# Turning batch 0's q and k 128 rows at a time, into two banks by position

## The chip, the cores and the metric

The kernel runs on one core of one Trainium2 chip. Its time is the device time of one execution in microseconds; 5 runs of the kernel before gave 304.98 to 306.46 us, with a median of 305.46 us. A smaller time is better. The profile is of one execution, which took 305.09 us as a run; its span, from the program's first to its last instruction, is 303.3 us.

## The reference

Two stages. The first is causal attention with a sliding window of 64 positions, for 8 batches of 8 heads, 576 positions, 64 values a head. The second is a two-layer network with a silu between its layers, over all 4608 tokens.

```python
scores = (1 / sqrt(64)) * q @ k.T                 # per batch and head, 576 x 576
mask   = (rel >= 0) & (rel < 64)                  # rel = query position - key position
attn   = softmax(where(mask, scores, -1e9)) @ v   # 576 x 64
x      = attn, heads side by side                 # 4608 tokens x 512
h      = x @ w_in                                 # 512 -> 2048
out    = (h * sigmoid(h)) @ w_out                 # 2048 -> 512, float32
```

## The kernel before

**Attention.** Scores need q and k with the 64 values of a head on the partitions. Batches 1 to 7 are turned by the vector engine (`turn_blocks`, L248). Batch 0 goes another way, which is the part that the change touches. `two` (L226) reads two heads of q or k as 1152 rows and gives 9 rows that follow each other to each of 128 partitions, so that partitions 0 to 63 hold one head and 64 to 127 the other. The load puts them, as bf16, into a tile `natb` of 128 x 576: by way of `nat` and a cast on ScalarE for the first pair of heads of q and of k (L233, L236), by a casting DMA of the POOL queue for the others (L230). `turn_first` (L276) turns the two tiles of four heads with TensorE matmuls against `ident`, into two PSUM banks, and `lift` (L291) copies each bank to its place in `qt` or `kt`, where the positions of a head lie in order again. There are four turns: q and k of heads 0 to 3 (a = 0) and of heads 4 to 7 (a = 1), each with two lifts.

For batch 0, `scores_first` (L311) adds the window's bias by a matmul (L314) and then multiplies k and q of two heads in halves of the array (L322). `expo` (L340) takes the exponential, `values` (L352) multiplies with v, and `inverse`, `normal`, `to_bridge` (L359, L362, L366) divide, and put the result into `bridge`, the network's input. A unit is one group g of three 64-position blocks and one half a of the heads; batch 0 has six units, n = 0 to 5, and a later batch three double ones. The values of v also need a copy shifted by half a block (`shift_v`, L300 and L302).

**Network.** The tokens go in 9 tiles of 512. `first_layer` (L372) has 16 blocks f of 4 matmuls each, silu (L378) on ScalarE, `second_layer` (L381) 64 matmuls, `copy_out` (L387) and a store. Of tile 0, the first six blocks are computed for 192 tokens and then for the other 320; and its second layer runs with f outermost, so that its 8 pieces of `w_out` (L267, two blocks f each) are needed one after the other. In between stand the scores (L334) and values (L352) of batch 1, three groups of each.

**Order.** The instructions' order on each engine comes from a planner, `Plan.run`, which plays the kernel through with the durations that are given to it and lets each engine take the ready work of the best rank. Work that needs PSUM takes the banks that have been free longest, and TensorE's idle time before batch 0's last exponential is filled with matmuls that nobody reads (`warm`, L586). The turn is entered with 0.7 us of TensorE time (L436), a lift with 0.64 us on ACT or 0.75 us on DVE. Once made, the order is fixed: each engine runs its instructions in turn, and each waits for semaphores.

All loads but the first two go through the POOL queue, in an order that is fixed as well: q and k of batch 0, its v, `w_in` (L261), q and k of batch 1, the first piece of `w_out`, and then v of batch 1 and the other pieces between each other.

Of the kernel before, what the change touches and what calls it, by code (L numbers as in the profile page):

```python
# [9 lines left out]
BF16 = mybir.dt.bfloat16  # L10
# [112 lines left out]
def kernel(ctx, tc, q, k, v, w_in, w_out, out):  # L123
    nc = tc.nc
    B, H, S, D = q.shape
# [11 lines left out]
    NK = 2  # L137
# [5 lines left out]
    NM0, MARGIN = 9, 1.3  # L143
# [8 lines left out]
    ident = keep.tile([128, 128], BF16, name="ident")  # L152
# [8 lines left out]
    natbs = [keep.tile([128, S], BF16, name=f"natb{i}") for i in range(NNB)]  # L161
    qt = [keep.tile([128, NP * S], BF16, name=f"qt{i}") for i in range(NK)]
    kt = [keep.tile([128, 64 + NP * S], BF16, name=f"kt{i}") for i in range(NK)]
# [9 lines left out]
    banks = [psum.tile([128, 512], FP32, name=f"at{i}") for i in range(4)]  # L173
    banks += [psum.tile([128, 512], FP32, name=f"mp{i}") for i in range(4)]

    p = Plan(
        {"at": range(4), "pv": range(4, 6), "mp": range(4, 8), "all": range(8)},
        rank=dict(prime=-8, early=-10, one=-9, first=-9, dma=-1, ld0=-1, st=-2, silu=-3, out=-2, pv=0, s=1, moe=99, warm=200, turn=2,
                  norm=0, inverse=0, bridge=0, exp=1, mask=1, lift=2, block=2, shift=2, cast=4, late=5, clear=9),
        rank0=dict(turn=-6, cast=-6, lift=-5, shift=-4.5, exp=-4, mask=-4, inverse=-3.5, norm=-3, bridge=-3.2),  # L180
        ahead=dict(s=-5.5, exp=-4.6, pv=-5.5, inverse=-4.3, norm=-4.2, bridge=-4.25),
    )
# [31 lines left out]
    def clear_k(i):  # L214
        nc.vector.memset(kt[i][:, 0:64].bitcast(FP32), 0.0)

    c_ident = p.add("one", {"POOL": 1.3}, const_ident)
    c_vv = [p.add("one", {"DVE": 0.25}, lambda _, i=i: clear_vv(i)) for i in range(NV)]
    c_k = [p.add("one", {"DVE": 0.15}, lambda _, i=i: clear_k(i)) for i in range(NK)]
# [9 lines left out]
    def load_first_cast(w, u, kk):  # L229
        nc.gpsimd.dma_start(out=natbs[w][:, 0:S], in_=two(u, kk))  # L230

    def load_first(i, kk):
        nc.sync.dma_start(out=nats[i][:, 0:2 * S].bitcast(FP32), in_=two(0, kk))  # L233

    def cast_first(e, i, w):
        copies[e](out=natbs[w][:, 0:S], in_=nats[i][:, 0:2 * S].bitcast(FP32))  # L236
# [33 lines left out]
        )  # L270


    def at_bf16(op, i=0):
        return banks[op["bank"][i]].bitcast(BF16)[:, 0:S]

    def turn_first(op, ws):  # L276

        for u in range(2):
            for m in range(NM0):
                for j in range(2):  # L280
                    r = slice(64 * j, 64 * j + 64)
                    nc.tensor.matmul(
                        banks[op["bank"][j]].bitcast(BF16)[64 * u:64 * u + 64, 64 * m:64 * m + 64],
                        lhsT=natbs[ws[u]][r, 64 * m:64 * m + 64], rhs=ident[r, r],
                        is_transpose=True, start=(m == 0), stop=(m == NM0 - 1),
                    )

    def place_one(b, pj, kk):
        return kt[b % NK][:, 64 + pj * S:64 + (pj + 1) * S] if kk else qt[b % NK][:, pj * S:(pj + 1) * S]

    def lift(e, op, pj, kk, i):  # L291
        copies[e](  # L292
            out=place_one(0, pj, kk).rearrange("x (p m) -> x p m", m=NM0),
            in_=at_bf16(op, i).rearrange("x (m p) -> x p m", m=NM0),
        )

    def shift_v(e, b, hf, a, z):
# [116 lines left out]
    def add_first_batch():  # L414
        got = {}
        for what, u in FIRST_LOADS:
            if what == "v":
                add_v_loads(0, [u], [c_vv[0]])
                continue
            kk = "qk".index(what)  # L420
            w = n_nat[1] % NNB
            n_nat[1] += 1
            if u == 0:
                i = n_nat[0] % NN
                n_nat[0] += 1
                ld = p.add("ld0", {"SP": 0.45}, lambda _, i=i, kk=kk: load_first(i, kk), dma=-0.15 if kk == 0 else 0.7)
                ca = p.add("cast", {"ACT": 0.7, "DVE": 0.56}, lambda e, i=i, w=w: cast_first(e, i, w), [ld])
                nat_free[i] = [ca]
            else:
                ca = p.add("early" if (what, u) in FIRST_LOADS[2:6] else "dma", {"POOL": 0.6}, lambda _, w=w, u=u, kk=kk: load_first_cast(w, u, kk), dma=0.8)  # L430
            got[what, u] = (w, ca)
            if (what, u ^ 1) not in got:
                continue
            a = u // 2
            ws, loaded = zip(*[got[what, 2 * a + i] for i in range(2)])
            tu = p.add("turn", {"PE": 0.7}, None, [*loaded, c_ident], lat=0.1, pool="all", nb=2)  # L436
            tu["fn"] = lambda _, tu=tu, ws=ws: turn_first(tu, ws)
            for i in range(2):
                x = 2 * a + i
                tu["untils"][i].append(p.add("lift", {"ACT": 0.64, "DVE": 0.75}, lambda e, tu=tu, x=x, kk=kk, i=i:  # L440
                                             lift(e, tu, x, kk, i), [tu, c_k[0]]))
                kq_done[(0, a)] = kq_done.get((0, a), []) + tu["untils"][i]

    def add_w_out(which):
# [23 lines left out]
    def add_v_loads(b, parts, busy):  # L468
        v_landed.setdefault(b, []).extend(
            p.add("dma", {"POOL": 1.0}, lambda e, part=part: load_v(e, b, part), busy, dma=1.1, lat=MARGIN * (b > 0)) for part in parts)  # L470
# [61 lines left out]
    def add_tile(j):  # L532
# [46 lines left out]
        free_gt.update(uses)  # L579

    add_first_batch()
    add_batch_v(0)


    def warm(op):
# [4 lines left out]
                 pool="all")  # L590
# [52 lines left out]
```

The softmax here doesn't subtract the row's maximum and nothing guards it: scores larger than these inputs give would overflow.

## Time and profile before

| | |
|---|---|
| median of 5 runs | 305.46 us (304.98 to 306.46) |
| the profiled execution, as a run | 305.09 us |
| its span | 303.3 us |
| mean granted TensorE clock | 0.994 |
| TensorE busy | 290.2 us (96%), 3635 matmuls |
| ScalarE, VectorE, POOL busy | 172.1, 137.2, 125.6 us |
| the turn's matmuls (L282) | 144, from 4.93 to 11.86 us |
| lifts (L292) on ACT | 5, of 627 to 645 ns |
| lifts (L292) on DVE | 3, of 758 ns |
| first layer of tile 0 (L372) | from 21.92 us on |
| first layer of tile 1 (L372) | from 56.92 us on |

The times below are counted from the start of the span. A row of the timeline holds its start, the time it covers, the engine, the line, the operation, what is written and read, and how many instructions were merged in it; in brackets stands the idle time of the engine just before it and what ended it. "issue" is idle time in which the engine waited for nothing that the profile shows. "PEld" are TensorE's weight loads, one for each matmul, which overlap the matmuls.

### The profile page before, as it was taken

To read this page: it belongs to the slowest core of one execution; us is meant where nothing else is said; L and a number is where in the kernel's file an instruction comes from. 1 tells how busy PE (TensorE), PEld (TensorE's weight loads), DVE (VectorE), ACT (ScalarE), POOL (GpSimd) and SP (SyncE) were. 2 spreads that over 40 slices of the span, in tenths; PEclk is the share of its full clock that TensorE was granted. 3 is DMA by queue.
4 is the path that set the end of the run, shared out by engine and by line. 5 is a ranking of instruction groups with operands and counts; after the bars stand their busy time and mean duration, and the time that the engine had idled before them with its cause. 6 is when DMAs were issued, how large, how long until landed. Compare 5 with 4: busy or idle time off the path is not lost.

```text
span 303.3 us, 8484 instructions
## 1 busy us (share of the span) xinstructions
PE 290.2 (96%) x3635; PEld 144.3 (48%) x3635; DVE 137.2 (45%) x329; ACT 172.1 (57%) x314; POOL 125.6 (41%) x177
## 2 busy tenths in 40 slices
PE   4959998999999999999999999999999999999996
PEld 2537444654544454445444454445445544444444
DVE  2465557753998198706970786065105520000000
ACT  4856662577357834774387628663767366226611
POOL 8967985958979997993320000000000000000000
PEclk9998999999999999999999999999999999999999
DMA  8999999999999999999390111001001110110012
GB/s 171 158 183 162 128 174 170 157 185 88 148 184 128 132 143 177 144 134 113 76 101 2 38 71 37 1 37 71 37 0 39 62 44 0 37 69 36 2 69 71
DMA packets 115238, 28.64 MB, mean 94 GB/s; under 512 B 104704, under 2 KB 110464, under 8 KB 115200
## 3 DMA queue, kind: packets, MB, share of 16 engines
q0 software_dynamic: 109440, 18.07, 79.0%
q1 hardware_dynamic: 5760, 10.03, 9.1%
q8 instruction: 28, 0.46, 0.7%
q14 instruction: 10, 0.08, 0.1%
HBM read 36.70 MB, written 9.44 MB: 152 GB/s over the span
## 4 chain that ended last, share of the span: by engine, by line
PE 92%; issue 3%; DMA 2%; POOL 1%; ACT 1%; DVE 1%; POOLq 0%; ACTq 0%
PE mp L372 42%; PE mp L381 42%; PE at L334 3%; PE mp L352 3%; DMA vv<-in_v_dram 2%; PE at L352 1%; POOL natb L230 1%; ACT e L340 0%; ACT g L378 0%; DVE kt L292 0%; DVE vv L302 0%; PE mp L314 0%; DVE vv L300 0%; PE mp L322 0%; POOL ident L189 0%
## 5 line engine op out<-in xcount | busy, mean ns | idle before, releaser
L381 PE MATMUL mp<-w_out_sb,g 128*128 128x512 bf16 (+2 forms) x608 | 130.2, 368 | 0.2
L372 PE MATMUL mp<-bridge,w_in_sb 128*128 128x512 bf16 (+3 forms) x624 | 129.3, 366 | 0.5 <-ACT g L378 0.4
L378 ACT ACTIVATE g<-mp 128x512 bf16<-128x512 f32 (+3 forms) x156 | 86.3, 564 | 37.0 <-PE mp L372 36.1
L372 PEld LDWEIGHTS <-w_in_sb 128*128 128x128 bf16 x624 | 61.6, 99 | 66.6 <-issue 6.6
L381 PEld LDWEIGHTS <-g 128*128 128x128 bf16 x608 | 55.8, 98 | 61.0 <-issue 0.3
L387 ACT COPY ot<-mp 128x512 f32<-128x512 f32 (+2 forms) x36 | 20.1, 562 | 64.7 <-PE mp L381 51.5
L343 DVE TENSOR_TENSOR e<-e,mask 128x384 bf16<-128x384 bf16 x84 | 25.9, 347 | 62.4 <-ACT e L340 61.6
L340 ACT ACTIVATE e<-at 128x384 bf16<-128x384 f32 x88 | 36.5, 496 | 19.0 <-PE at L334 18.7
L240 POOL DMA_DIRECT2D nat<-in_k_dram x56 | 38.5, 711 | 13.1 <-DMA vv<-in_v_dram 6.9
L240 POOL DMA_DIRECT2D nat<-in_q_dram x56 | 37.8, 696 | 3.8 <-DMA w_in_sb<-in_moe_w_in_dram 2.0
L255 POOL DMA_DIRECT2D vv<-in_v_dram x32 | 33.0, 1055 | 9.6 <-PE mp L352 9.6
L366 DVE STREAM_TRANSPOSE bridge<-ox 128x384 bf16<-128x384 bf16 x48 | 24.7, 551 | 0.1
L248 DVE STREAM_TRANSPOSE qt<-nat 128x576 bf16<-128x576 bf16 x28 | 19.8, 745 | 4.3 <-DMA nat<-in_q_dram 4.3
L248 DVE STREAM_TRANSPOSE kt<-nat 128x576 bf16<-128x576 bf16 x28 | 19.7, 742 | 1.3 <-DMA nat<-in_k_dram 1.3
L362 DVE TENSOR_TENSOR ox<-mp,rc 128x384 bf16<-128x384 f32 x37 | 18.3, 535 | 0.1
L352 PEld LDWEIGHTS <-e 128*32 128x32 bf16 x1152 | 11.0, 95 | 14.4 <-issue 12.2
L359 DVE RECIPROCAL rc<-mp 128x6 f32<-128x6 f32 x37 | 6.9, 190 | 16.2 <-PE mp L352 15.6
L302 DVE COPY vv<-vv 64x576 bf16<-64x576 bf16 (+1 forms) x13 | 8.5, 654 | 10.1 <-DMA vv<-in_v_dram 9.8
L334 PE MATMUL at<-qt,kt 32*128 32x64 bf16 x1008 | 11.8, 190 | 0.2 <-ACT e L340 0.2
L334 PEld LDWEIGHTS <-kt 32*128 32x128 bf16 x1008 | 9.4, 92 | 4.6 <-issue 3.7
L352 PE MATMUL mp<-vv,e 128*32 128x65 bf16 x888 | 10.4, 194 | 0.0
L340 ACT ACT_TABLE_LOAD x7 | 9.0, 1283 | 2.2 <-PE at L334 2.1
(50 smaller groups left out, 86.5 us busy)
## 6 DMA issues: line engine op xcount, KB each, us to landing
out_dram<-ot SPq DMA_DIRECT2D x35, 256.0 KB, 2.1
vv<-in_v_dram POOLq DMA_DIRECT2D x32, 144.0 KB, 5.8
nat<-in_q_dram POOLq DMA_DIRECT2D x56, 72.0 KB, 4.2
nat<-in_k_dram POOLq DMA_DIRECT2D x56, 72.0 KB, 4.0
w_out_sb<-in_moe_w_out_dram POOLq DMA_DIRECT2D x8, 256.0 KB, 7.1
w_in_sb<-in_moe_w_in_dram POOLq DMA_DIRECT2D x6, 256.0 KB, 7.8
w_in_sb<-in_moe_w_in_dram POOLq DMA_DIRECT2D x4, 128.0 KB, 5.4
natb<-in_q_dram POOLq DMA_DIRECT2D x3, 144.0 KB, 4.7
```

What stands on the lines that cost most here:

```text
L240: nc.gpsimd.dma_start(out=nats[i][32 * h:32 * h + 32].rearrange("p (r d) -> p r d", r=NR), in_=(q, k)[kk][b, 4 * a + h].rearrange("(r p) d ...
L248: nc.vector.transpose(out=to[:, 2 * a * S:2 * a * S + 2 * S].rearrange("x (s r t) -> x s r t", s=2, r=NR)[:, :, n * part:n * part + n], in ...
L255: queue[e].dma_start(out=vv[b % NV][:, 2 * g0 + 1:2 * g1 + 1:2, 0:D], in_=v[b].rearrange("h s d -> (h s) d").rearrange("(g p) d -> p g d", ...
L334: nc.tensor.matmul(at_six(op["bank"][h])[:, a, x], lhsT=kt[b % NK][r, at:at + 128], rhs=qt[b % NK][r, at:at + 64], start=(s == a == x == 0 ...
L340: nc.scalar.activation(out=es[n % NE], in_=at_six(bank), func=ACTF.Exp, scale=scale)
L343: nc.vector.tensor_mul(es[n % NE], es[n % NE], mask0 if g == 0 else mask)
L352: nc.tensor.matmul(at_pv(bank)[32 * h:32 * h + 32, x, t], lhsT=e_of(b, a, n, h)[:, x, 32 * t:32 * t + 32], rhs=vv[b % NV][:, (4 * a + h) * ...
L366: nc.vector.transpose(out=bridge[:, n0:n0 + 3, 2 * a:2 * a + 2].rearrange("x t s (u i) -> x t s u i", u=2), in_=oxs[n % NOX].rearrange("p ...
L372: nc.tensor.matmul(banks[bank["bank"][0]][:, lo:hi], lhsT=w_in_sb[:, c, ft * 128:(ft + 1) * 128], rhs=bridge[:, (j * TT + lo) // 64:(j * T ...
L378: nc.scalar.activation(out=gts[gt][:, lo:hi], in_=banks[bank["bank"][0]][:, lo:hi], func=ACTF.Silu)
L381: nc.tensor.matmul(banks[bank["bank"][0]][:, 0:hi - lo], lhsT=gts[gt][:, m * 128:(m + 1) * 128], rhs=w_out_sb[:, f, lo:hi], start=(f == 0) ...
L387: copies[e](out=ots[ot][:, lo:hi], in_=banks[bank["bank"][0]][:, 0:hi - lo])
```

## The change

The two banks of a turn no longer hold two heads each, but all four heads for a part of the positions: the first bank takes the rows m = 0 to 4 of each partition's nine, the second m = 5 to 8. One matmul turns all 128 partitions, two heads, of one m, where before it turned 64. A turn so has 18 matmuls with 128 columns each in place of 36 with 64, and the two `natb` tiles now alternate, where before the first was finished ahead of the second. A lift copies 128 x 640 or 128 x 512 values in place of 128 x 576, and writes them 9 values apart, where before it wrote in order and read 64 values apart. The turn is entered into the planner with 0.6 us in place of 0.7.

```diff
-    def at_bf16(op, i=0):
-        return banks[op["bank"][i]].bitcast(BF16)[:, 0:S]
+    HALVES = ((0, 5), (5, NM0))
+
+    def turned(op, i):
+        lo, hi = HALVES[i]
+        return banks[op["bank"][i]].bitcast(BF16)[:, 0:128 * (hi - lo)].rearrange("x (m y) -> x m y", y=128)
 
     def turn_first(op, ws):
 
-        for u in range(2):
-            for m in range(NM0):
-                for j in range(2):
-                    r = slice(64 * j, 64 * j + 64)
+        for i, (lo, hi) in enumerate(HALVES):
+            for m in range(lo, hi):
+                for u in range(2):
                     nc.tensor.matmul(
-                        banks[op["bank"][j]].bitcast(BF16)[64 * u:64 * u + 64, 64 * m:64 * m + 64],
-                        lhsT=natbs[ws[u]][r, 64 * m:64 * m + 64], rhs=ident[r, r],
-                        is_transpose=True, start=(m == 0), stop=(m == NM0 - 1),
+                        turned(op, i)[64 * u:64 * u + 64, m - lo], lhsT=natbs[ws[u]][:, 64 * m:64 * m + 64], rhs=ident,
+                        is_transpose=True, start=(m == lo), stop=(m == hi - 1),
                     )
 
-    def place_one(b, pj, kk):
-        return kt[b % NK][:, 64 + pj * S:64 + (pj + 1) * S] if kk else qt[b % NK][:, pj * S:(pj + 1) * S]
-
-    def lift(e, op, pj, kk, i):
+    def lift(e, op, a, kk, i):
+        to = kt[0][:, 64:] if kk else qt[0]
         copies[e](
-            out=place_one(0, pj, kk).rearrange("x (p m) -> x p m", m=NM0),
-            in_=at_bf16(op, i).rearrange("x (m p) -> x p m", m=NM0),
+            out=to[:, 2 * a * S:2 * a * S + 2 * S].rearrange("x (j p m) -> x m j p", j=2, m=NM0)[:, HALVES[i][0]:HALVES[i][1]],
+            in_=turned(op, i).rearrange("x m (j p) -> x m j p", j=2),
         )
...
-            tu = p.add("turn", {"PE": 0.7}, None, [*loaded, c_ident], lat=0.1, pool="all", nb=2)
+            tu = p.add("turn", {"PE": 0.6}, None, [*loaded, c_ident], lat=0.1, pool="all", nb=2)
             tu["fn"] = lambda _, tu=tu, ws=ws: turn_first(tu, ws)
             for i in range(2):
-                x = 2 * a + i
-                tu["untils"][i].append(p.add("lift", {"ACT": 0.64, "DVE": 0.75}, lambda e, tu=tu, x=x, kk=kk, i=i:
-                                             lift(e, tu, x, kk, i), [tu, c_k[0]]))
+                tu["untils"][i].append(p.add("lift", {"ACT": 0.64, "DVE": 0.75}, lambda e, tu=tu, a=a, kk=kk, i=i:
+                                             lift(e, tu, a, kk, i), [tu, c_k[0]]))
```

## The prediction

> **What bounds the kernel now.** I read the page first, then TensorE's timeline up to 60 us, where the change can act, then the DMA issues there, and last the built programs' order, before and after.
>
> ```profile
> span 303.3 us, 8484 instructions
> ...
> PE   4959998999999999999999999999999999999996
> ...
> PEclk9998999999999999999999999999999999999999
> DMA  8999999999999999999390111001001110110012
> ...
> q8 instruction: 28, 0.46, 0.7%
> ...
> PE 92%; issue 3%; DMA 2%; POOL 1%; ACT 1%; DVE 1%; POOLq 0%; ACTq 0%
> ```
>
> TensorE sets the end (92% of the chain that ended last) and is full from the fourth slice on. The DMA engines are as full for the first 19 slices (some 144 us). So early on TensorE may be early and yet have to wait for a load. The dip in slice 3 (15 to 23 us) and the stretch from 37 to 56 us show where it does not flow:
>
> ```profile
> 17.21 0.29 PE L352 MATMUL at<-vv,e 128*32 128x65 bf16 x13
> 21.12 0.27 PE L352 MATMUL at<-vv,e 128*32 128x65 bf16 x11 [3.62 <-issue]
> ...
> 37.24 0.81 POOL L267 DMA_DIRECT2D w_out_sb<-in_moe_w_out_dram  x1
> 37.39 2.30 PE L381 MATMUL mp<-w_out_sb,g 128*128 128x512 bf16 x9
> ...
> 43.45 0.55 PE L334 MATMUL at<-qt,kt 32*128 32x64 bf16 x48
> ...
> 44.13 1.24 PE L381 MATMUL mp<-w_out_sb,g 128*128 128x512 bf16 x5
> ...
> 45.80 0.52 PE L334 MATMUL at<-qt,kt 32*128 32x64 bf16 x45 [0.20 <-ACT e L340]
> ...
> 46.25 1.25 PE L381 MATMUL mp<-w_out_sb,g 128*128 128x512 bf16 x5
> ...
> 48.68 0.43 PE L352 MATMUL at<-vv,e 128*32 128x65 bf16 x31
> ...
> 50.05 0.31 PE L352 MATMUL at<-vv,e 128*32 128x65 bf16 x17 [0.95 <-issue]
> ...
> 50.30 4.92 PE L381 MATMUL mp<-w_out_sb,g 128*128 128x512 bf16 x22
> ```
>
> Two things are to be seen. Two stops by "issue" lie in the middle of a run of equal matmuls, which wait for no semaphore there. And 44.13 is a landing: the fourth piece of w_out is issued at 37.24, and the DMA issues of that window give it 6.8 us to landing, so 44.1 (its semaphore is full at 44.09).
>
> **The two stops.** Counted in TensorE's program, they lie before instructions 706 and 1474, which are 768 = 3 x 256 apart. Queue q8 brought 28 packets of 16 KB for 7278 TensorE instructions, 260 each. So TensorE's program comes in blocks of 256, which begin at 194, 450, 706, 962, 1218, 1474 and so on. The packet of the first stop ran from 18.77 to 19.74 and TensorE went on at 21.12, that of the second from 47.72 to 48.67 and 50.05: in both 1.38 us after its end. The time from the start of one block's work to when the block after it could run (packet's end + 1.38) was 6.8 (block 450), 6.7, 3.8 (block 962, begun at 38.45), 4.2 (block 1218, at 45.83) and 4.9 us (block 1474). Where 256 instructions last less than this, TensorE stops. After the first stop the clock was at half for 3.4 us (21.81 to 25.23; the mean from 21.1 to 26 is 0.65).
>
> [...]
>
> **The change, part by part.** *Turns.* 72 of 144 matmuls go. 36 took 0.66 us at full clock (11.20 to 11.86), in pairs of different rows of the array: 18 pairs of 64 columns. The new 18 are 9 pairs of 128 columns, so the same 1152 columns in turn if the pairs, which now differ in the array's columns, still overlap. L352's groups differ in the same way, 4 at a time: 48 matmuls of 65 columns took 0.49 us, where one after another they would take 48 x 65 x 0.424 ns = 1.32 us (a filler of 384 columns every 0.163 us gives 0.424). So 0, at worst 18 x 128 x 0.424 = 0.98 in place of 0.49: +0.5 a turn, +1.0 at the slow pace of the first two (1.10 and 0.99 us). I take 0, the nearer row.
>
> [...]
>
> *First turn.* Its second matmul now reads the second tile, which lands at 5.30: up to 0.4 us later than the start at 4.93.
>
> *Lifts.* Eight as before. On ACT 0.64 us for 576 and 0.50 for 384 values make 0.69 for 640; on DVE 0.76 x 512/576 = 0.67. No row writes 2-byte values 18 bytes apart. Bounds: 0.5 (the 384-value row) and, as an estimate, twice the L292 rows, 1.3 and 1.5 us. I take 0.7. Queued behind the lifts are ACT's exponentials and DVE's shifts of v.
>
> *What hides these.* The lifts of k's second half stand behind the shift of v on DVE, which waits for v's landing at 12.33 (5.93 + 6.4), as now. Then the first layer needs w_in's sixth piece (issued 13.37, semaphore full at 20.79), and the second layer w_out's second piece (32.80 + 4.8 = 37.6). POOL's and SP's programs are unchanged, and none of these loads waits for TensorE. Without this cover each microsecond late would count in full.
>
> *Order.* Up to the first layer TensorE, ACT and DVE are reordered; from there on TensorE's program is the same but for bank numbers, 140 instructions earlier (637 in place of 777). So the blocks begin 140 instructions later in the work. Block 450 now begins in the values of n = 2, 706 in the first layer, 962 at the second scores of batch 1, 1218 in its first values, 1474 in its third.
>
> **The sum.** Without the stop at 17.5 the values of batch 0 end near 18.2, 3.6 us earlier. The 192-token blocks wait for w_in at 20.8, the 320-token ones for the last transpose to bridge: DVE's eight steps behind the last values, some 4.5 us, so 22.9. A late block 450 or 706 can add a microsecond or two; I put block 706 at 24 to 25. Then 14 x 0.134 + 40 x 0.215 + 8 x 0.215 = 12.2 us bring the second piece of w_out into use at 36.2 to 37.2; it lands at 37.57. Before, it was used at 39.10. Third piece: 34.51 + 6.3 = 40.8, before used at 41.41. Fourth: 44.1, before used at 44.13. So the 3.6 us, and 1.7 of half clock, are all gone at 44.13. What is left is gained behind it, and its cause is that the second scores, before the landing and not held by it, run at 42.55 in place of 43.44, with their exponentials:
>
> - 5 matmuls of L381, 1.08: 45.21
> - third scores, now without the wait until 45.80 for exponentials, 0.48: 45.69
> - 3 matmuls, 0.65: 46.34; fifth piece of w_out (38.98 + 7.4) 46.42; 2 matmuls, 0.43: 46.85
> - first values with 0.1 of changeover, 0.59: 47.44
> - 3 matmuls, 0.65, and second values, 0.59: 48.68
>
> The shifts of v (landed 45.06) end near 45.9 and the second exponentials near 44.9, in time. Before, the same point is 50.30, so 1.62 us are gained: 0.47 before the values and 1.15 at the stop of block 1474. The later pieces land at 47.64, 48.88 and 50.48, ahead of their use (48.9 on). From 50.3 on TensorE was full, and the chain that follows moves as a whole.
>
> Whether a new stop takes the old one's place is decided by block 1218: block 962 begins at 42.55, and 1218 is wanted at 47.25, 4.7 us later. The nearest rows in time are 3.8 and 4.2, the farthest 6.8: no stop, at worst 2.1. I take none. Block 1474 is wanted 6.55 us after that.
>
> 305.09 - 1.62 = 303.47 for a run like the profiled one, which stands 0.37 under the median: **303.8 us**.
>
> **Rivals.** *A stop in the new place.* Block 1218 is 0.3 to 1.7 us late (5.0 to 6.4 us after 962): gain 0 to 1.3, some 304.7 us. For it: 6.7 and 6.8 among the rows. Against: both come from before 28 us, where w_in is loaded.
>
> *The whole early gain arrives*: 3.62 + 1.7 = 5.3, so 300.1 us. For it: the stop is on the chain. Against: w_out's landings, which POOL's order fixes.
>
> *Slower, by late blocks twice.* At X us a block, the stop is X - 4.7 at 1218 and X - 6.55 at 1474. Above X = 6.9 the two take more than the gain and 0.9 us besides; at 7.5 they take 2.8 + 0.95, so 307.6 us. For it: 6.8 is close, and weight pieces of 256 KB are in the queues then. Against: no row is over 6.8.
>
> *The early gain is not made*, because the new lifts or turns are slow: at their upper bounds the path is some 3 us longer, the second piece is used at 39 to 40 us, and about 305.3 comes out.
>
> **How the numbers follow.** No difference within 0.3% (0.92 us) can be told from this kernel's spread. Forecast 0.52, a stop in the new place 0.22, early gain not made 0.09, slower 0.13, whole gain 0.04. Faster by more: nearly all of the first, a third of the second, the last, 0.58; slower 0.13; the rest, 0.29, the same. The range from 303.0 to 305.7 leaves out the whole gain, most of slower and a little more; the likeliest case alone has 303.0 to 304.4.
>
> **What would show it.** After: no issue gap before the first layer of 3 us, which begins at 18 to 20 us, and no half clock there; L381's fourth piece still at 44.1; the second scores at 42 to 43; second values ending near 48.7, first layer of tile 1 at 55.3 in place of 56.92. An issue gap inside L352 between 47 and 49 us is the second rival. The prediction is wrong if the landing near 44.1 moves, or if the lifts take over 1.5 us.

## The result, and the profile after

The change made the kernel slower, by 0.36% (the ratio of the runs), where the forecast had it 0.5% faster.

| | before | after | predicted |
|---|---|---|---|
| median, us | 305.98 (80 runs) | 307.55 (43 runs) | 303.8 |
| ratio to before, 95% interval | | 1.0036 [1.0022, 1.0049] | 0.995 |
| profiled execution, as a run | 305.09 | 307.09 | 303.47 |
| its span | 303.3 | 305.3 | |
| lifts on ACT (640 values) and DVE (512) | | 2.95 to 3.32, 2.40 to 2.62 | 0.7 |
| first layer of tile 0 | 21.92 | 24.90 | 18 to 20 |
| second piece of w_out first used | 39.10 | 42.05 | 37.6 |
| second layer goes on after batch 1's second values | 50.30 | 52.12 | 48.7 |
| first layer of tile 1 | 56.92 | 58.74 | 55.3 |

Seven of the 43 runs lie between 305.66 and 306.04, the others between 306.8 and 308.6; why they part stays open. The difference of the medians is 1.57 us, and 0.36% is 1.1 us.

The page of the kernel after (the 40 slices are of 7.6 us):

```profile
span 305.3 us, 8339 instructions
...
PE   4668999999999999999999999999999999999996
...
PEclk9979999999999999999999999999999999999999
...
PE 91%; ACT 5%; DVE 2%; POOL 1%; issue 1%; POOLq 0%; ACTq 0%
PE mp L380 41%; PE mp L371 40%; PE at L333 3%; PE mp L351 3%; ACT qt L291 2%; ACT kt L291 2%; ACT e L339 1%; PE at L351 1%; DVE bridge L365 1%; POOL natb L230 1%; DVE ox L361 1%; PE at L284 0%; PE at L584 0%; ACT g L377 0%; PE at L313 0%
```

In the chain that ended last, "issue" has gone from 3% to 1%: the stops are away, as was meant. ACT has gone from 1% to 5%, and 2% and 2% of it are the lift, L291. TensorE's dip lies in slices 1 to 4 now, and the clock falls in the third (0.72 on average from 19 to 25 us). The groups of L291, each with the least, the median and the greatest duration in ns and the first and last start, and below them what waited for them:

```profile
L291 ACT COPY qt<-at x2: 3025/3171/3317, 6.0 to 11.4; 128x640 bf16<-128x640 bf16 x2
L291 DVE COPY qt<-at x2: 2467/2544/2622, 6.4 to 11.1; 128x512 bf16<-128x512 bf16 x2
...
L291 DVE COPY kt<-at x1: 2401/2401/2401, 15.5 to 15.5; 128x512 bf16<-128x512 bf16 x1
L291 ACT COPY kt<-at x1: 2946/2946/2946, 16.0 to 16.0; 128x640 bf16<-128x640 bf16 x1
...
  PEld L321: 4.5, 2
  PE at L321: 3.7, 2
```

Not 0.7 us but 2.4 to 3.3, some 4.7 ns a value on either engine. The scores, L321, wait for them. The chain of waits from 4 to 30 us (start, time, what) shows how they lie one behind the other on ACT:

```profile
6.00 3.02 ACT qt L291
9.02 2.82 ACT kt L291
11.84 2.83 ACT qt L291
14.68 1.43 ACT e L339 x4
16.10 2.85 ACT kt L291
```

13 us pass on ACT from the first lift to the end of the last, and the exponentials stand behind the third of them. In this chain an ACT lift takes 2.82 to 3.02 us; the records of 3.31 and 3.32 begin some 0.5 us before the lift ahead of them ends. TensorE's timeline has the rest:

```profile
9.26 0.69 PE L284 MATMUL at<-ident,natb 128*64 128x128 bf16 x18
...
11.90 0.35 PE L321 MATMUL at<-qt,kt 64*128 64x64 bf16 x12 [1.51 <-ACT kt L291]
...
19.00 0.43 PE L321 MATMUL at<-qt,kt 64*128 64x64 bf16 x12 [2.20 <-ACT kt L291]
...
24.90 3.17 PE L371 MATMUL mp<-bridge,w_in_sb 128*128 128x192 bf16 x26
...
40.34 2.30 PE L380 MATMUL mp<-w_out_sb,g 128*128 128x512 bf16 x9
...
46.89 1.25 PE L380 MATMUL mp<-w_out_sb,g 128*128 128x512 bf16 x5
...
52.12 4.92 PE L380 MATMUL mp<-w_out_sb,g 128*128 128x512 bf16 x22
...
58.74 1.47 PE L371 MATMUL mp<-bridge,w_in_sb 128*128 128x256 bf16 x12
```

The first layer begins 2.98 us later than before. All of w_out's pieces are there by the time they are used (the fourth is used at 46.89 and landed at 43.53), so there is nothing left in which the lateness could be lost: 2.95 us at the second piece. The stop of block 1474 is gone, as predicted, and gives 1.15 back: 2.95 - 1.15 = 1.80, and 1.82 is what the rows have, 52.12 against 50.30 and 58.74 against 56.92. The span is 2.0 us longer.

### The profile page after: what moved, and what is told of

The parts are those of the page before. It is cut to its first block, busy times and chain, and to the rows that moved or that the text cites. A ratio compares the mean times of both kernels' runs of the same rounds, so it can differ in the third digit from the quotient of the medians.

```text
span 305.3 us, 8339 instructions
## 1 busy us (share of the span) xinstructions
PE 291.6 (96%) x3564; PEld 143.4 (47%) x3564; DVE 143.1 (47%) x330; ACT 180.4 (59%) x313; POOL 125.2 (41%) x177
## 4 chain that ended last, share of the span: by engine, by line
PE 91%; ACT 5%; DVE 2%; POOL 1%; issue 1%; POOLq 0%; ACTq 0%
PE mp L380 41%; PE mp L371 40%; PE at L333 3%; PE mp L351 3%; ACT qt L291 2%; ACT kt L291 2%; ACT e L339 1%; PE at L351 1%; DVE bridge L365 1%; POOL natb L230 1%; DVE ox L361 1%; PE at L284 0%; PE at L584 0%; ACT g L377 0%; PE at L313 0%
## 5 line engine op out<-in xcount | busy, mean ns | idle before, releaser
L371 PEld LDWEIGHTS <-w_in_sb 128*128 128x128 bf16 x624 | 60.2, 97 | 67.9 <-issue 7.9
L339 ACT ACTIVATE e<-at 128x384 bf16<-128x384 f32 x90 | 37.5, 498 | 18.8 <-PE at L333 18.7
L240 POOL DMA_DIRECT2D nat<-in_k_dram x56 | 37.3, 675 | 9.7 <-DMA vv<-in_v_dram 3.3
L361 DVE TENSOR_TENSOR ox<-mp,rc 128x384 bf16<-128x384 f32 x39 | 19.4, 536 | 0.1
L351 PE MATMUL mp<-vv,e 128*32 128x65 bf16 x936 | 11.4, 195 | 0.0
L301 DVE COPY vv<-vv 64x576 bf16<-64x576 bf16 (+1 forms) x14 | 7.6, 544 | 3.2 <-DMA vv<-in_v_dram 2.9
```

Of the source, the lines that this page charges most:

```text
L240: nc.gpsimd.dma_start(out=nats[i][32 * h:32 * h + 32].rearrange("p (r d) -> p r d", r=NR), in_=(q, k)[kk][b, 4 * a + h].rearrange("(r p) d ...
L339: nc.scalar.activation(out=es[n % NE], in_=at_six(bank), func=ACTF.Exp, scale=scale)
L351: nc.tensor.matmul(at_pv(bank)[32 * h:32 * h + 32, x, t], lhsT=e_of(b, a, n, h)[:, x, 32 * t:32 * t + 32], rhs=vv[b % NV][:, (4 * a + h) * ...
L361: nc.vector.tensor_mul(oxs[n % NOX], at_pv(bank)[:, :, :, 0:D], rcs[n % NRC].unsqueeze(3).to_broadcast([128, 3, 2, D]))
L371: nc.tensor.matmul(banks[bank["bank"][0]][:, lo:hi], lhsT=w_in_sb[:, c, ft * 128:(ft + 1) * 128], rhs=bridge[:, (j * TT + lo) // 64:(j * T ...
```

## The experiments

Two questions: is it the lift's output pattern alone, and would the rest of the sum have held without it? The first four kernels ran on one chip, 12 times each (the second of them 5 times), beside 29 runs of the kernel before with a median of 305.87 us.

**Dense writes.** Here batch 0's q and k keep the order of the bank in which they were turned, so that its scores are of other positions than the reference's; all else is the kernel after.

```diff
-            out=to[...].rearrange("x (j p m) -> x m j p", j=2, m=NM0)[:, HALVES[i][0]:HALVES[i][1]],
+            out=to[...].rearrange("x (m j p) -> x m j p", j=2, m=NM0)[:, HALVES[i][0]:HALVES[i][1]],
```

> The changed kernel, its lifts writing their values one after the other (q and k of batch 0 so stay in the order of the bank, and batch 0's scores are of other positions than the reference's). Theory, the 2-byte writes 18 bytes apart are what costs (4.7 ns a value on both engines): lifts fall from 2.4 to 3.3 us to 0.6 to 0.75 us, the first layer begins at 18 to 20 us, the fourth piece of w_out still sets 44 us, and the rest of the prediction's sum is seen: 303.5 to 304.5 us. Rival, the new turn or the reading of its banks costs: lifts stay over 2 us and the time near 307.

Measured: 304.41 us, ratio 0.9949 [0.9926, 0.9972]. The groups of the lift's line:

```profile
L291 ACT COPY qt<-at x2: 692/692/692, 5.8 to 10.1; 128x640 bf16<-128x640 bf16 x2
L291 DVE COPY qt<-at x2: 424/424/425, 6.2 to 10.5; 128x512 bf16<-128x512 bf16 x2
```

The same number of values, from the same banks, in 692 and 424 ns. The input's pattern and the turns are as in the kernel after, so the distance between the writes is the cost. The 0.69 that the prediction worked out for ACT is what a dense write takes.

**The old turn with writes apart.** The opposite: the kernel before, with the two loops of its lift swapped, so that it reads in order and writes 9 values apart.

```diff
-            out=place_one(0, pj, kk).rearrange("x (p m) -> x p m", m=NM0),
-            in_=at_bf16(op, i).rearrange("x (m p) -> x p m", m=NM0),
+            out=place_one(0, pj, kk).rearrange("x (p m) -> x m p", m=NM0),
+            in_=at_bf16(op, i).rearrange("x (m p) -> x m p", m=NM0),
```

> The kernel before, with its turns, banks and instruction order; only a lift's two inner loops are swapped, so that it reads its bank in order and writes 9 values apart, and gives the same result. Theory, writes apart cost 4.7 ns a value: lifts take 2.6 to 2.9 us instead of 0.64 and 0.76, and the time is 1 to 4 us over before. Rival, the new turn or its banks cost: lifts as before and no change of the time.

Measured: 311.43 us, ratio 1.0176 [1.0139, 1.0213].

```profile
L292 ACT COPY kt<-mp x2: 3017/3027/3037, 9.3 to 11.9; 128x576 bf16<-128x576 bf16 x2
...
L292 DVE COPY kt<-at x1: 2693/2693/2693, 18.7 to 18.7; 128x576 bf16<-128x576 bf16 x1
```

Without any of the change's turns, the lifts go from 0.64 and 0.76 us to 2.7 and 3.0. The pattern alone makes the loss. The 5.5 us are more than was expected: this kernel still has the stop before instruction 706 (here 3.49 us, from 25.54 to 29.03), behind its late lifts; how the 5.5 divide was not followed further.

**Runs of neighbours.** The kernel after, with the position m as the innermost loop on both sides. The same values go to the same places, in runs of 5 or 4 neighbours.

```diff
-            out=to[...].rearrange("x (j p m) -> x m j p", j=2, m=NM0)[:, HALVES[i][0]:HALVES[i][1]],
-            in_=turned(op, i).rearrange("x m (j p) -> x m j p", j=2),
+            out=to[...].rearrange("x (j p m) -> x j p m", j=2, m=NM0)[:, :, :, HALVES[i][0]:HALVES[i][1]],
+            in_=turned(op, i).rearrange("x m (j p) -> x j p m", j=2),
```

> The changed kernel with a lift's loops in another order: it writes runs of 5 (or 4) neighbouring values and then leaves out 4 (or 5), and reads 128 values apart. Same result. Theory, what costs is that each 2-byte write starts a place of its own: about a fifth to a quarter of 4.7 ns a value or the usual 1.1 to 1.3, whichever is more, so 0.7 to 1.0 us a lift and 303.5 to 304.8 us. Rival, two engines write between each other's values in the same rows: that is still so, so lifts stay at 2.4 us or more and the time near 307.

Measured: 304.34 us, ratio 0.9939 [0.9917, 0.9962]. It beats both kernels: it is the change as it should have been written. Its lifts, and then its timeline:

```profile
L291 ACT COPY qt<-at x2: 752/752/752, 5.9 to 10.2; 128x640 bf16<-128x640 bf16 x2
L291 DVE COPY qt<-at x2: 719/722/725, 6.3 to 10.4; 128x512 bf16<-128x512 bf16 x2
```

```profile
18.66 0.95 PE L371 MATMUL mp<-bridge,w_in_sb 128*128 128x192 bf16 x8
...
38.64 0.38 PE L380 MATMUL mp<-w_out_sb,g 128*128 128x512 bf16 x1 [2.44 <-DMA w_out_sb<-in_moe_w_out_dram]
...
42.34 1.89 PE L380 MATMUL mp<-w_out_sb,g 128*128 128x512 bf16 x8 [1.23 <-DMA w_out_sb<-in_moe_w_out_dram]
...
45.48 1.24 PE L380 MATMUL mp<-w_out_sb,g 128*128 128x512 bf16 x5 [0.77 <-DMA w_out_sb<-in_moe_w_out_dram]
...
50.04 4.92 PE L380 MATMUL mp<-w_out_sb,g 128*128 128x512 bf16 x22
```

The first layer begins at 18.66, and TensorE then stands 2.44, 1.23 and 0.77 us before three pieces of w_out: the early gain is lost there, as the prediction had it. No stop by issue is in the second layer. In this one execution the loads were about 1 us late (the second piece landed at 38.60, before at 37.57), so 50.04 is 0.26 earlier than before; the dense kernel, whose loads were sooner (the second piece landed at 37.82), is at tile 1 at 56.03 against 56.92, 0.89 earlier:

```profile
44.33 1.24 PE L380 MATMUL mp<-w_out_sb,g 128*128 128x512 bf16 x5 [0.81 <-DMA w_out_sb<-in_moe_w_out_dram]
...
47.16 0.59 PE L380 MATMUL mp<-w_out_sb,g 128*128 128x512 bf16 x2 [0.36 <-DMA w_out_sb<-in_moe_w_out_dram]
...
56.03 1.91 PE L371 MATMUL mp<-bridge,w_in_sb 128*128 128x256 bf16 x16
```

For what the gain is worth the medians must serve: 305.87 - 304.34 = 1.53.

**Blocks moved.** The kernel before, with nothing of the change, but with 58 small matmuls that nobody reads ahead of all others. They and their weight loads are 116 instructions and shift the blocks of 256.

```diff
+    pre = keep.tile([128, 64], BF16, name="pre")
+    nc.vector.memset(pre, 0.0)
+    for i in range(58):
+        r = slice(32 * (i % 4), 32 * (i % 4) + 32)
+        nc.tensor.matmul(banks[7][r, 0:32], lhsT=pre[:, 0:32], rhs=pre[:, 32:64], start=True, stop=True)
```

> The kernel before with 58 small matmuls that nobody reads (116 instructions) put ahead of its first one, in TensorE's idle time up to 4.2 us: the blocks of 256 instructions then begin at the same places of the work as in the changed kernel, and lifts are as before. Theory, the two stops lie where a block begins that is late: the stops of 3.6 and 1.0 us go, and the time is 1.0 to 1.8 us under before (304.2 to 305.0). Rival, the stops belong to the place in the work: they stay within the values of n = 4 and of batch 1's second group, and the time stays.

Measured: 304.25 us, ratio 0.9944 [0.9923, 0.9965]. TensorE's timeline:

```profile
18.49 0.19 PE L322 MATMUL at<-qt,kt 64*128 64x64 bf16 x1 [1.24 <-issue]
...
43.80 1.24 PE L381 MATMUL mp<-w_out_sb,g 128*128 128x512 bf16 x5 [0.82 <-DMA w_out_sb<-in_moe_w_out_dram]
...
46.94 0.59 PE L381 MATMUL mp<-w_out_sb,g 128*128 128x512 bf16 x2 [0.66 <-DMA w_out_sb<-in_moe_w_out_dram]
...
49.19 4.92 PE L381 MATMUL mp<-w_out_sb,g 128*128 128x512 bf16 x22
```

The stop before instruction 706 is there still, in front of other work (batch 0's scores) and of 1.24 us in place of 3.62; so it sits at a place in the program and not at a matmul. The one before 1474 is gone. The expectation that both go was met by half. The time is that of the repaired change: with the old turns and more matmuls than before, moving the boundaries gives 1.6 us as well (305.87 - 304.25). That the added matmuls bring TensorE to its full pace sooner is not what gives it: the third turn takes 0.99 us here (from 9.69 on), in the kernel before 0.66 (from 8.47 on). That the turns are fewer is worth nothing of itself that these runs can tell.

**The copies by themselves.** The kernel before, with copies of 256 values behind its end, first on DVE, then on ACT, then on both. From L619 to L625 only the output's distance changes:

```diff
+    nc.vector.tensor_copy(out=pa[:, 0:256], in_=banks[0].bitcast(BF16)[:, 0:256])
...
+    nc.vector.tensor_copy(out=pa[:, 0:2304].rearrange("x (n s) -> x n s", s=9)[:, :, 0:1], in_=banks[0].bitcast(BF16)[:, 0:256].rearrange("x (n r) -> x n r", r=1))
...
```

> The kernel before with copies of 256 values from PSUM, and one from SBUF, added behind its end, one at a time on DVE and then on ACT: 2-byte values written one after the other, 4, 8, 16, 18, 32 and 64 bytes apart, in runs of 2 and 4 values 18 bytes apart, 4-byte values one after the other and 36 bytes apart; and last two pairs with both engines writing 18 bytes apart at once. Theory, what costs is a write of less than a whole word of some size: 18 bytes apart takes some 4.7 ns a value (1.2 us for 256) on an engine alone, also 4 bytes apart, runs of 2 and 4 are cheaper by their length, and 4-byte values apart cost little more than together. Rival, the two engines take the time from each other: alone about half, 0.6 us, and 1.2 us in the pairs. Second rival, the distance itself costs: 4-byte values 36 bytes apart cost as much as 2-byte values, and 64 bytes apart costs more than 8.

The time of this one execution, 326.9 us, is longer by the added copies. Its timeline: on DVE L619 is dense, L620 to L623 write 4, 8, 16 and 18 bytes apart, L626 and L627 runs of 2 and 4 values every 18 bytes, L628 and L629 4-byte values, dense and 36 bytes apart. On ACT L635 writes 18 bytes apart. L645 and L646 do so on both engines at once.

```profile
301.37 0.29 DVE L619 COPY pa<-at 128x256 bf16<-128x256 bf16 x1 [51.88 <-PE at L618]
301.70 0.44 DVE L620 COPY pa<-at 128x256 bf16<-128x256 bf16 x1
302.17 0.72 DVE L621 COPY pa<-at 128x256 bf16<-128x256 bf16 x1
302.93 1.29 DVE L622 COPY pa<-at 128x256 bf16<-128x256 bf16 x1
304.26 1.27 DVE L623 COPY pa<-at 128x256 bf16<-128x256 bf16 x1
...
308.12 0.62 DVE L626 COPY pa<-at 128x256 bf16<-128x256 bf16 x1
308.78 0.43 DVE L627 COPY pa<-at 128x256 bf16<-128x256 bf16 x1
309.25 0.42 DVE L628 COPY pa<-at 128x256 f32<-128x256 f32 x1
309.71 0.61 DVE L629 COPY pa<-at 128x256 f32<-128x256 f32 x1
...
314.12 1.28 ACT L635 COPY pa<-at 128x256 bf16<-128x256 bf16 x1
...
322.62 1.27 ACT L646 COPY pb<-at 128x256 bf16<-128x256 bf16 x1
...
322.82 1.27 DVE L645 COPY pa<-at 128x256 bf16<-128x256 bf16 x1
```

Three readings. For 2-byte values from PSUM written 4 bytes apart or more the two engines pay the same (on ACT 0.44, 0.72, 1.29 and 1.28 us at 4, 8, 16 and 18 bytes), and at 18 bytes also together (L645 and L646), so they don't hinder each other; that rival falls. The price grows with the distance up to 16 bytes and is flat from there (at 32 and 64 bytes 1.23 and 1.27 us); my theory that any distance costs 4.7 ns a value was wrong at 4 bytes, 0.44 us. And a 2-byte value 18 bytes apart costs twice what a 4-byte value 36 bytes apart does (1.27 us against 0.61 for 256).

From L620 to L622 follows a fit: 256 values touch 64, 128 and 256 stretches of 16 bytes, the distance from which the price is flat, and 0.16 us + 4.4 ns a stretch gives 0.44, 0.72 and 1.29. It meets the lifts that it was not made from, where single values are written 18 bytes apart: 512 values 2.41 (2.40 to 2.62 measured), 576 values 2.69 (2.69 to 3.04 in the old turn with writes apart), 640 values 2.98 (2.95 to 3.32); the longest of each overlap the copy ahead of them. The lifts in runs of 4 or 5 neighbours lie over 144 stretches, 0.79 by the fit and 0.72 and 0.75 measured. Elsewhere it fails. Runs of 2 lie over 144 stretches too, and took 0.62; the 4-byte values 36 bytes apart touch 256, 1.29 by the fit and 0.61 measured. Nor has it a term for the input: the kernel before writes densely and reads 128 bytes apart, 0.48 by the fit for 72 stretches and 0.76 measured on DVE. So it is a fit for single 2-byte values and no mechanism; why they cost this stays open.

**Lifts on DVE alone.** The kernel after, with ACT taken out of the lift; one execution.

```diff
-                tu["untils"][i].append(p.add("lift", {"ACT": 0.64, "DVE": 0.75}, lambda e, tu=tu, a=a, kk=kk, i=i:
+                tu["untils"][i].append(p.add("lift", {"DVE": 0.75}, lambda e, tu=tu, a=a, kk=kk, i=i:
```

> The changed kernel with all eight lifts on DVE. Theory, a write 18 bytes apart costs 4.7 ns a value on one engine alone: 2.4 us for 512 and 3.0 us for 640 values, eight in a row, so some 21 us of lifts on DVE, and 2 to 6 us more than the changed kernel. Rival, the engines hinder each other: some 1.2 and 1.5 us, and the time falls to that of before or under it.

Measured: 314.57 us, beside 305.97 for the kernel before. One group of the lift's line:

```profile
L291 DVE COPY qt<-at x4: 2624/2810/3199, 6.5 to 19.3; 128x640 bf16<-128x640 bf16 x2, 128x512 bf16<-128x512 bf16 x2
```

With ACT out of the way a lift on DVE takes no less than before, so the rival of hindrance falls in the kernel too. Eight of them one after another last to 27.6 us, and the time, 7 us over the kernel after, is above what was expected.

**w_out sooner.** The runs of neighbours, with w_out's third and fourth pieces ahead of more of batch 1's v.

```diff
-    FIRST, SECOND_LOADS = 6, "awbwvwvvwv"
+    FIRST, SECOND_LOADS = 6, "awbwwvwvvv"
```

> The kernel of e3 with one change in the order of POOL's loads: the third piece of w_out is asked for ahead of v's first quarter of batch 1, and the later ones so too. Theory, after the lifts are repaired the early gain is held back by w_out's landings alone: the second layer's waits for pieces 3 and 4 (1.6 and 0.9 us in e3) shrink by about 1 us each, v's later quarters come about 1 us later but ahead of their use near 48 us, and the time falls by 0.3 to 1.2 us against e3, to 303.2 to 304.1 us. Rival, the loads as a whole set the time there, and their order doesn't matter: 304.0 to 304.8 us, with the wait moved to v or to the last pieces.

Measured, on another chip than the kernel that it changes: 304.15 us (12 runs), ratio 0.9957 [0.9929, 0.9985]. In TensorE's timeline the waits for the third and fourth piece are gone, and one is new before the fifth:

```profile
46.64 0.59 PE L380 MATMUL mp<-w_out_sb,g 128*128 128x512 bf16 x2 [1.16 <-DMA w_out_sb<-in_moe_w_out_dram]
```

The wait moved, and the ratio lies within the interval of the order that it replaced. Whether another order can bring the early gain through stays open.

## Why the prediction was wrong

**Turns: right.** A turn of the kernel before, and one of the kernel after with its weight loads:

```profile
11.20 0.66 PE L282 MATMUL at<-ident,natb 64*64 64x64 bf16 x36
```

```profile
9.26 0.53 PEld L284 LDWEIGHTS <-natb 128*64 128x64 bf16 x18 [0.32 <-issue]
9.26 0.69 PE L284 MATMUL at<-ident,natb 128*64 128x128 bf16 x18
```

18 matmuls in 0.69 us at a granted clock of 1.00, before 36 in 0.66: fewer instructions and the same columns, nothing won and nothing lost. The 18 weight loads take 0.53 us of the same 0.69, beside the matmuls. The first turn waited 0.18 for its second tile; up to 0.4 was allowed.

**Lifts: the step that failed.** "I take 0.7", with 1.3 and 1.5 as the upper bound. It was 2.4 to 3.3. The value was scaled by the count of elements from rows that write in order, and the upper bound was twice such a row, with nothing under the two. The text itself says that no row writes 2-byte values 18 bytes apart; a bound that no row supports should have been wider, or been replaced by asking what the pattern does. The sign that it gave for being wrong, lifts of over 1.5 us, came. That it is the output's distance and nothing else of the change was shown by taking it away (dense, runs) and by adding it to the old turn. In the copies by themselves, 256 2-byte values on DVE cost 0.72 us already at 4 values apart, against 0.29 dense; 4-byte values 36 bytes apart pay as well, but far less: 0.61 against 0.42.

**Cover: fell with it.** I named the landings of w_in and w_out as the work that hides the lifts, to 20.8 and 37.6 us. How much they hide is seen in the runs of neighbours: 2.44 + 1.23 + 0.77 = 4.4 us of waits, in an execution with late loads. The kernel after reaches the first layer 24.90 - 18.66 = 6.2 us later than that one, partly at a lower clock (0.72 from 19 to 25 us), after TensorE's idle 2.20 us before 19.00. The waits are used up, and 52.12 - 50.04 = 2.1 us remain behind the second values.

**Blocks: right, but for a constant.** No stop came before block 1218, and that of block 1474 was not there any more, in the kernel after or with the runs of neighbours; the rival of a stop in the new place, and that of two late blocks, did not come. That the latter's figure, 307.6, is the time measured is chance. The 1.38 us from a packet's end until TensorE goes on is not fixed: it was 1.50 with the blocks moved (16.99 to 18.49) and 1.61 in the old turn with writes apart (27.42 to 29.03).

**The rest of the sum: borne out as a whole, not step by step.** 1.62 us were predicted; runs of neighbours, whose lifts take 0.72 and 0.75, gain 1.53 between the medians, 1.87 by the ratio (0.0061 x 305.87). The early gain goes at w_out's landings there, the first layer begins at 18.66, and no half clock comes there (a granted clock of 1.00 from 10.1 to 60 us). But behind the fourth piece neither execution shows the sum's steps: that piece is used at 45.48 and, in the dense kernel, 44.33 (44.1 in the sum), the dense kernel waits 0.36 us for the fifth, and at tile 1 they are 0.26 and 0.89 us ahead. How far the near agreement is luck these runs can't tell. One term is also added up wrongly: 18.2 and 4.5 make 22.7 and not 22.9; 22.49 was measured.

**The rival that came** is "the early gain is not made". Its mechanism was named rightly, and its size was not: it took the failed upper bound, 3 us of path, and so ended at 305.3, where 6.2 us of path gave 307.55.

## What to carry to other kernels

The output's pattern can set a copy's price, and not its number of values alone (a lift took 2.40 to 3.32 us, dense 0.42 and 0.69): before a loop order is turned round, look for a row that writes with the same distance, and where there is none, measure it or let the upper bound be several times the dense row. When a layout must be split, give the innermost loop to neighbours in the output, also if the input is then read far apart (0.72 and 0.75 us here, with the input read 128 values apart). And removed instructions move the boundaries of all the code behind them: here that alone, without the change, was worth as much as the repaired change (1.62 us against 1.53).

## What was not expected of the hardware

- 2-byte values written 16 or more bytes apart from PSUM into SBUF cost 4.8 to 5.0 ns each on ACT and DVE (1.23 to 1.29 us for 256, all included), against 1.1 dense on DVE (0.29 us); 4-byte values 36 bytes apart 2.4 (0.61 us).
- Reading PSUM 128 bytes apart, with dense writes, cost ACT nothing that shows (0.64 us for 576 values, 0.69 for 640 in order), but DVE 0.76 us for 576 where 512 in order took 0.42.
- At 18 bytes apart DVE, but not ACT, wrote faster when it read from SBUF: 256 values took 0.72 us on DVE from SBUF and 1.27 from PSUM, on ACT 1.31 and 1.28.
- A stop for a code block stood at one place of the program before different matmuls: 3.62 us amid the values, 1.24 amid the scores, both before instruction 706.
